# Banded attention followed by a two-layer feed-forward: 64-key tiles, longer load rows, a second load queue and a column-split last tile

## The chip, the cores and the metric

The kernel runs on one core of a Trainium2 chip. Its time is device microseconds (us) of one execution. The names of the engines are those of the profile: PE multiplies matrices (TensorE), PEld loads its weights, ACT is ScalarE, DVE is VectorE, POOL is GpSimd, SP is SyncE. A "unit" is one step of attention, a "block" a run of tokens that goes through the feed-forward together.

## The reference

Eight sequences of 576 tokens, eight heads of 64; attention reaches 32 tokens to each side. The 4608 x 512 result goes through a feed-forward with a squared relu. All inputs and the output are float32. Cut to what matters:

```python
def _attn_ref(q, k, v):                       # each (8, 8, 576, 64)
    scores = (1 / np.sqrt(D)) * np.matmul(q, k.transpose(0, 1, 3, 2))
    mask = np.abs(pos[:, None] - pos[None, :]) <= 32
    ...                                       # softmax over the masked scores
    return np.matmul(attn, v)

def _moe_ref(x, w_in, w_out, s, b):           # x (4608, 512), w_in (512, 2048), w_out (2048, 512)
    r = np.maximum(x @ w_in, 0.0)
    g = s * (r * r) + b
    return g @ w_out                          # s and b are single numbers
```

The constant b is taken out of the product: the kernel adds b times the column sums of w_out at the end.

## The kernel before

All work is declared as tasks. A planner with assumed durations puts them in an order, each engine runs its list, and semaphores join the lists. Loads bring one block of tokens with all heads, so that every contiguous piece in memory is one token of one head, 256 bytes:

```python
        def load(b, n, blk, stream="sp", waits=()):
            ...
                lambda e: e.dma_start(
                    STG[n][p0:p1, blk, :].rearrange("p (h d) -> p h d", h=H),
                    src_of[n][b, :, s0:s0 + ns, :].rearrange("h s d -> s h d"),
                ),
```

Weights come through GpSimd's queue, which casts them to bfloat16 on the way. A unit is 192 queries of four heads, with 128 keys a tile, so there are 8 x 3 x 2 = 48. Its softmax sums are a matrix product with ones, and the division is exp(-ln(sum)) on ACT:

```python
        def unit(b, t, g2, after):
            ...
                        fns.append(lambda e, u=u, pr=pr, a=a, hh=hh: e.matmul(
                            SC[:, hh, 256 * u + 128 * a:256 * u + 128 * a + 128],
                            lhsT=KT[slot][64 * hh:64 * hh + 64, pr, q0 + 128 * a:q0 + 128 * a + 128],
                            rhs=QT[slot][64 * hh:64 * hh + 64, pr, q0 + 64 * a:q0 + 64 * a + 128],
                            start=True, stop=True))
            ...                                # exp on ACT with bias=ZERO_F[:, :], mask on DVE
            for (dst, res) in ((SS, "SS"), (AV, "AV")):
                ...                            # SS: lhs = ONES, AV: lhs = VB; 8 matmuls each
            add("act", lambda e: e.activation(LNS[e_][:, :], SS[:, 0:384], AF.Ln,
                                              bias=ZERO_F[:, :], scale=1.0),
            ...
            add("act", lambda e: e.activation(REC[e_][:, :], LNS[e_][:, :], AF.Exp,
                                              bias=ZERO_F[:, :], scale=-1.0),
            ...                                # DVE: XT = AV * REC
```

The feed-forward takes blocks of 384, 128 and then 512 tokens. A first product (w_in), relu on ACT, square on DVE, and a second product (w_out) a 128-token tile at a time:

```python
    sizes = [384, 128]
    while sum(sizes) < T:
        sizes.append(min(512, T - sum(sizes)))
    ...
        for m in range(NM + 1):
            if m < NM:
                for ft in range(16):
                    s1(m, ft)
            if m == 0:
                colsum()
            else:
                for sub in range(TBLK[m - 1][1] // 128):
                    for qd in range(4):
                        s2(m - 1, sub, qd)
```

The softmax here doesn't subtract the row's maximum and nothing guards it: scores larger than these inputs give would overflow.

Of the kernel before, what the change touches and what calls it, by code (L numbers as in the profile page):

```python
# [17 lines left out]
NBLK = (S + 127) // 128  # L18
KCOLS = NBLK * 128
TOK = 512  # L20
# [4 lines left out]
class _Task:  # L25


    __slots__ = ("n", "stream", "fns", "cost", "lat", "key", "deps", "after", "users", "left",
                 "ready", "start", "fin", "dma", "sem", "seq", "val", "used", "snap")

    def __init__(self, n, stream, fns, cost, lat, key, dma):
        self.n, self.stream, self.fns, self.cost, self.lat, self.key, self.dma = \
            n, stream, fns, cost, lat, key, dma
        self.deps, self.after, self.users = set(), [], []
        self.ready = self.start = self.fin = 0.0
        self.sem = self.seq = self.val = None
        self.used = False
        self.snap = None


class _Graph:
# [3 lines left out]

    STREAMS = ("pe", "act", "dve", "pool", "sp")
    LAT = {"pe": 230.0, "act": 110.0, "dve": 90.0, "pool": 120.0, "sp": 60.0}

    def __init__(self, queues):
        self.queues = queues  # L50
        self.tasks = []
        self.writer, self.readers, self.named = {}, {}, {}

    def add(self, stream, fns, cost, reads=(), writes=(), key=0.0, accum=False, dma=None, waits=(),
            after=(), name=None, lat=None):


        if not isinstance(fns, list):
            fns = [fns]
        t = _Task(len(self.tasks), stream, fns, cost, self.LAT[stream] if lat is None else lat, key,  # L60
                  dma)
        t.deps.update(waits)
        for r in reads:
            assert r in self.writer, r
            t.deps.add(self.writer[r])
# [6 lines left out]
        t.after = list(after)  # L72
# [6 lines left out]
        if name is not None:  # L79
            self.named[name] = t  # L80
        self.tasks.append(t)
        return t

    def plan(self):
        free = {s: 0.0 for s in self.STREAMS}
        dma_free = 0.0
        for t in self.tasks:
            aft = [self.named[a] for a in t.after]
            t.left = len(t.deps) + len(aft)
            for d in t.deps:  # L90
                d.users.append((t, True))
            for d in aft:
                d.users.append((t, False))
        open_ = {s: [] for s in self.STREAMS}
        for t in self.tasks:
            if t.left == 0:
                open_[t.stream].append(t)
        order = []
        while len(order) < len(self.tasks):
            best = None  # L100
            for s in self.STREAMS:
                for t in open_[s]:
                    c = (max(free[s], t.ready), t.key, t.n)
                    if best is None or c < best[0]:
                        best = (c, t)
            assert best is not None, "a cycle"
            (st, _, _), t = best
            open_[t.stream].remove(t)
            t.start = st
            free[t.stream] = st + t.cost  # L110
            if t.dma is not None:
                dma_free = max(dma_free, st + 1300.0) + t.dma[1]
                t.fin = dma_free + 700.0
            else:
                t.fin = st + t.cost
            order.append(t)
            for u, hard in t.users:
                u.left -= 1
                if hard and u.stream == t.stream and t.dma is None and t.stream == "pe":
                    r = t.fin  # L120
                elif hard:
                    r = t.fin + (100.0 if t.dma is not None else t.lat)
                else:
                    r = t.start
                u.ready = max(u.ready, r)
                if u.left == 0:
                    open_[u.stream].append(u)
        self.order = order

    def emit(self, sems):  # L130


# [5 lines left out]
        plan = []  # L138

# [12 lines left out]
        for t in self.order:  # L152
            s = t.stream
            need = {}
            for d in t.deps:
                if s == "pe" and d.stream == "pe" and d.dma is None:
                    continue
                want(s, d, need)
            if t.dma is not None:
# [20 lines left out]
        count = {}  # L180
        for t, waits in plan:
            if t.dma is not None:
# [6 lines left out]
            def run(eng, t=t, waits=waits):  # L189
                for d in waits:  # L190
                    eng.wait_ge(sems[d.sem], d.val)
                for i, fn in enumerate(t.fns):
                    ins = fn(eng)
                    if t.dma is not None:
# [15 lines left out]
def bass_sliding_window_symmetric__then__act_starrelu_kernel(  # L210
# [12 lines left out]
    NT3 = S // 192  # L223

    sizes = [384, 128]
# [8 lines left out]
    with ExitStack() as es:  # L234
# [6 lines left out]
        def ps(shape, nm, dt=F32):  # L241
            uid["n"] += 1
            return es.enter_context(nc.psum_tensor(f"{nm}_{uid['n']}", list(shape), dt))

        WIN_BF = sb((128, 4, DFF), BF16, "win")
        WOUT_BF = sb((128, 16, DM), BF16, "wout")
        XT = sb((128, NPAIR, T), BF16, "xt")
        STG = {n: sb((128, NBLK, DM), F32, "stg" + n) for n in "qk"}
        STG["v"] = sb((128, 2 * NT3, DM), F32, "stgv")
        NAT = {n: sb((128, NBLK, DM), BF16, "nat" + n) for n in "qk"}  # L250
        VB = [sb((128, 2 * NT3, DM), BF16, "vb") for _ in range(2)]
        QT = [sb((128, NPAIR, S), BF16, "qt") for _ in range(2)]
        KT = [sb((128, NPAIR, S + 2 * WIN), BF16, "kt") for _ in range(2)]
        EX = [sb((128, 2, 512), BF16, "ex") for _ in range(2)]
        MASK = sb((128, 2, 512), BF16, "mask")
        LNS = [sb((128, 384), F32, "lns") for _ in range(2)]
        REC = [sb((128, 384), F32, "rec") for _ in range(2)]
        ONES = sb((128, 3, 64), BF16, "ones")
        ONESW = sb((128, 128), BF16, "onesw")
        IDENT = sb((128, 128), BF16, "ident")  # L260
        ZERO_F = sb((128, 1), F32, "zero")
        GT = [sb((128, 16, 512), BF16, "gt") for _ in range(2)]
        R1 = [sb((128, 512), BF16, "r1") for _ in range(4)]
        OUTS = [sb((128, DM), F32, "outs") for _ in range(3)]
# [3 lines left out]
        W = [ps((128, 512), "w") for _ in range(2)]  # L268
        O = [ps((128, 512), "o") for _ in range(2)]
        SC = ps((128, 2, 512), "sc")  # L270
        AV = ps((128, 512), "av")
        SS = ps((128, 512), "ss")
        BANKS = {("W", 0): W[0], ("W", 1): W[1], ("O", 0): O[0], ("O", 1): O[1]}

        queues = {"w": [f"dmaW{i}" for i in range(10)], "l": [f"dmaL{i}" for i in range(24)],
                  "a": [f"dmaA{i}" for i in range(8)], "o": [f"dmaO{i}" for i in range(8)],
                  "t": [f"dmaT{i}" for i in range(8)]}
        names = list(_Graph.STREAMS) + [x for n in queues for x in queues[n]]
# [4 lines left out]
        def rows(blk):  # L283
            return min(128, S - blk * 128)


        src_of = {"q": q, "k": k, "v": v}

        def load(b, n, blk, stream="sp", waits=()):
            if n == "v":  # L290
                k0 = 192 * (blk // 2) - WIN + 128 * (blk % 2)
                p0, p1 = max(0, -k0), min(128, S - k0)
                s0 = k0 + p0
            else:
                p0, p1 = 0, rows(blk)
                s0 = 128 * blk
            ns = p1 - p0
            return add(
                stream,
                lambda e: e.dma_start(  # L300
                    STG[n][p0:p1, blk, :].rearrange("p (h d) -> p h d", h=H),
                    src_of[n][b, :, s0:s0 + ns, :].rearrange("h s d -> s h d"),
                ),
                1070.0 if stream != "pool" else 1900.0, writes=[("STG", n, blk)],
                key=16 * (b - 2), waits=waits,
# [337 lines left out]
```

## Time and profile before

| | before |
|---|---|
| time, median of 3 runs | 375.03 us (374.42 to 376.37) |
| span of the profiled run | 373.8 us |
| PE busy / idle | 319.2 / 54.6 us |
| first feed-forward matmul starts | 31.88 us |
| first 512-token block starts | 99.25 us |
| DMA packets, of them under 512 B | 127,869 / 116,672 |

Here are two more views of the kernel before. The first is the page's line of busy times. The second is the trace cut into three stretches at the start of the first 512-token block and at the end of PE's work: each line has the stretch, its length, then busy time and instruction count of PE, PEld, DVE, ACT and POOL, then granted PE clock, DMA share and GB/s.

```profile
PE 319.2 (85%) x2385; PEld 155.5 (42%) x2424; DVE 193.2 (52%) x439; ACT 206.4 (55%) x310; POOL 44.7 (12%) x62
```

```profile
0.00:99.25 99.25, 59.11 (x533) 34.88 (x538) 48.41 (x127) 44.42 (x74) 26.35 (x41) 0.88 1.13 192
99.25:370.20 270.95, 260.05 (x1853) 120.62 (x1886) 144.09 (x312) 162.00 (x236) 18.37 (x22) 0.99 0.65 123
370.20:373.80 3.60, 0.00 (x0) 0.00 (x0) 0.75 (x1) 0.00 (x0) 0.00 (x0) 0.80 0.19 73
```

The busy line alone says "PE 85%". The stretches say more: 40 of the 54.6 idle microseconds lie in the first 99.25 (99.25 - 59.11), where the DMA share is full and the clock is 0.88. In the second stretch PE is busy 96%, so there less PE work can help, and at most 11 us of idle.

### The profile page before, as it was taken

The numbers are of one execution on the slowest core, as the hardware profiler recorded it, in microseconds if no ns is written. First come the engines' busy times: TensorE is split into PE (matmuls) and PEld (weight loads), VectorE is DVE, ScalarE is ACT, GpSimd is POOL, SyncE is SP. The second block draws the span as 40 slices with busy tenths as digits, with TensorE's granted clock in tenths as the row PEclk, the third lists the DMA queues.
The fourth block names the chain that finished last, engine by engine and source line by source line (L and its number), as shares of the span: only waits on it lengthen the run. The fifth ranks groups of instructions, "written<-read, shape, count | busy, mean of one in ns | idle before, by whom it ended". The sixth has DMA issues, their size and how long they took to land.

```text
span 373.8 us, 6108 instructions
## 1 busy us (share of the span) xinstructions
PE 319.2 (85%) x2385; PEld 155.5 (42%) x2424; DVE 193.2 (52%) x439; ACT 206.4 (55%) x310; POOL 44.7 (12%) x62
## 2 busy tenths in 40 slices
PE   1277985935499999988898899989999999999996
PEld 0144543523244444443444344434444444444442
DVE  4363525745556775676585586454444453333321
ACT  1266732255368678767677576657676764434300
POOL 3012241342221210121111000000000000000000
PEclk9999998975599999999999999999999999999999
DMA  8979999999999999999899798863000001001012
GB/s 164 208 110 187 190 225 206 202 190 213 230 221 147 180 200 231 186 198 193 188 172 213 132 174 174 189 141 89 28 31 31 28 30 56 28 30 56 28 58 84
DMA packets 127869, 52.71 MB, mean 141 GB/s; under 512 B 116672, under 2 KB 120768, under 8 KB 127840
## 3 DMA queue, kind: packets, MB, share of 16 engines
q1 hardware_dynamic: 113648, 36.32, 54.2%
q0 software_dynamic: 7424, 14.29, 19.8%
q10 hardware_dynamic: 6768, 1.70, 2.7%
q8 instruction: 19, 0.31, 0.4%
q14 instruction: 10, 0.08, 0.1%
HBM read 38.80 MB, written 9.44 MB: 129 GB/s over the span
## 4 chain that ended last, share of the span: by engine, by line
PE 54%; DMA 19%; SPq 9%; DVE 7%; ACTq 3%; ACT 3%; issue 2%; DVEq 0%
PE o L543 25%; PE w L525 22%; DMA stgq<-in_q_dram 12%; DMA stgk<-in_k_dram 7%; SPq L300 6%; ACTq L300 3%; SPq L387 3%; PE ss L458 3%; PE sc L435 2%; DVE ex L445 2%; PE av L458 2%; ACT ex L442 1%; DVE xt L472 1%; DVE vb L379 1%; DVE gt L534 1%
## 5 line engine op out<-in xcount | busy, mean ns | idle before, releaser
L525 PE MATMUL w<-xt,win 128*128 128x512 bf16 (+2 forms) x624 | 146.4, 367 | 5.5 <-DVE xt L472 4.2
L543 PE MATMUL o<-wout,gt 128*128 128x512 bf16 x554 | 141.5, 382 | 6.0 <-DVE cvec L567 4.0
L525 PEld LDWEIGHTS w<-xt,win 128*128 128x128 bf16 x640 | 59.4, 100 | 71.8 <-issue 5.1
L543 PEld LDWEIGHTS o<-wout,gt 128*128 128x128 bf16 x576 | 53.2, 98 | 65.5 <-DVE cvec L567 4.2
L442 ACT ACTIVATE ex<-sc,zero 128x1024 bf16<-128x1024 f32 x48 | 53.2, 1109 | 12.1 <-PE sc L435 12.1
L445 DVE TENSOR_TENSOR ex<-ex,mask 128x1024 bf16<-128x1024 bf16 x48 | 33.0, 688 | 33.2 <-ACT ex L442 32.7
L300 POOL DMA_DIRECT2D stgv<-in_v_dram x42 | 35.7, 853 | 120.5 <-DVE vb L379 111.5
L465 ACT ACTIVATE lns<-ss,zero 128x384 f32<-128x384 f32 x48 | 27.7, 578 | 27.6 <-PE ss L458 27.5
L531 ACT ACTIVATE r_29<-w,zero 128x512 bf16<-128x512 f32 (+2 forms) x40 | 25.7, 643 | 30.7 <-PE w L525 30.6
L458 PE MATMUL ss<-ex,ones 128*64 128x128 bf16 x384 | 22.1, 244 | 20.5 <-DVE ex L445 20.1
L531 ACT ACTIVATE r_28<-w,zero 128x512 bf16<-128x512 f32 (+2 forms) x40 | 25.7, 642 | 23.1 <-PE w L525 22.6
L531 ACT ACTIVATE r_31<-w,zero 128x512 bf16<-128x512 f32 (+2 forms) x40 | 25.7, 644 | 23.0 <-PE w L525 22.0
L531 ACT ACTIVATE r_30<-w,zero 128x512 bf16<-128x512 f32 (+2 forms) x40 | 25.7, 643 | 19.2 <-PE w L525 18.8
L555 DVE SCALAR_TENSOR_TENSOR outs<-o,sb_36,cvec 128x512 f32<-128x512 f32 x36 | 26.8, 746 | 13.2 <-PE o L543 12.8
L472 DVE TENSOR_TENSOR xt<-av,rec 128x384 bf16<-128x384 f32 x48 | 26.5, 552 | 11.5 <-ACT rec L468 11.2
L379 DVE CAST natq<-stgq 128x512 bf16<-128x512 f32 (+1 forms) x40 | 17.2, 432 | 25.3 <-DMA stgq<-in_q_dram 25.0
L458 PEld LDWEIGHTS ss<-ex,ones 128*64 128x64 bf16 x384 | 13.6, 119 | 39.6 <-DVE ex L445 26.7
L468 ACT ACTIVATE rec<-lns,zero 128x384 f32<-128x384 f32 x48 | 29.3, 610 | 0.8
L435 PE MATMUL sc<-qt,kt 64*128 64x128 bf16 x384 | 21.2, 237 | 9.0 <-ACT qt L407 5.3
L534 DVE TENSOR_TENSOR gt<-r_29 128x512 bf16<-128x512 bf16 (+2 forms) x40 | 15.8, 396 | 22.7 <-ACT r_29 L531 22.7
L534 DVE TENSOR_TENSOR gt<-r_31 128x512 bf16<-128x512 bf16 (+2 forms) x40 | 15.8, 396 | 22.3 <-ACT r_31 L531 22.0
L534 DVE TENSOR_TENSOR gt<-r_30 128x512 bf16<-128x512 bf16 (+2 forms) x40 | 15.8, 394 | 18.6 <-ACT r_30 L531 18.6
(43 smaller groups left out, 134.4 us busy)
## 6 DMA issues: line engine op xcount, KB each, us to landing
out_dram<-outs SPq DMA_DIRECT2D x36, 256.0 KB, 2.3
stgq<-in_q_dram SPq DMA_DIRECT2D x31, 256.0 KB, 5.8
stgk<-in_k_dram SPq DMA_DIRECT2D x29, 256.0 KB, 6.0
stgv<-in_v_dram POOLq DMA_DIRECT2D x28, 256.0 KB, 5.7
stgv<-in_v_dram POOLq DMA_DIRECT2D x14, 192.0 KB, 5.9
win<-in_moe_w_in_dram POOLq DMA_DIRECT2D x4, 512.0 KB, 6.4
wout<-in_moe_w_out_dram POOLq DMA_DIRECT2D x4, 512.0 KB, 5.8
stgq<-in_q_dram SPq DMA_DIRECT2D x8, 128.0 KB, 5.9
```

What stands on the lines that cost most here:

```text
L300: lambda e: e.dma_start(STG[n][p0:p1, blk, :].rearrange("p (h d) -> p h d", h=H), src_of[n][b, :, s0:s0 + ns, :].rearrange("h s d -> s h d ...
L435: fns.append(lambda e, u=u, pr=pr, a=a, hh=hh: e.matmul(SC[:, hh, 256 * u + 128 * a:256 * u + 128 * a + 128], lhsT=KT[slot][64 * hh:64 * h ...
L442: add("act", lambda e: e.activation(EX[e_][:, :, :], SC[:, :, :], AF.Exp, bias=ZERO_F[:, :], scale=0.125), 1130.0, reads=["SC", "ZERO"], w ...
L445: add("dve", lambda e: e.tensor_tensor(EX[e_][:, :, :], EX[e_][:, :, :], MASK[:, :, :], ALU.mult), 700.0, reads=[("E", e_), "MASK"], write ...
L458: fns.append(lambda e, u=u, a=a, hh=hh, dst=dst, lhs=lhs: e.matmul(dst[64 * hh:64 * hh + 64, 192 * u + 64 * a:192 * u + 64 * a + 128], lhs ...
L465: add("act", lambda e: e.activation(LNS[e_][:, :], SS[:, 0:384], AF.Ln, bias=ZERO_F[:, :], scale=1.0), 600.0, reads=["SS", "ZERO"], writes ...
L468: add("act", lambda e: e.activation(REC[e_][:, :], LNS[e_][:, :], AF.Exp, bias=ZERO_F[:, :], scale=-1.0), 600.0, reads=[("LNS", e_), "ZERO ...
L472: add("dve", lambda e: e.tensor_tensor(XT[:, prs[0]:prs[1] + 1, x0:x0 + 192], AV[:, 0:384].rearrange("p (u c) -> p u c", u=2), REC[e_][:, ...
L525: add("pe", [lambda e, kc=kc: e.matmul(W[wb][:, 0:nt], lhsT=WIN_BF[:, kc, ft * 128:(ft + 1) * 128], rhs=XT[:, kc, t0:t0 + nt], start=(kc = ...
L531: add("act", lambda e: e.activation(R1[rb][:, 0:nt], W[wb][:, 0:nt], AF.Relu, bias=ZERO_F[:, :], scale=1.0), 280 + 0.82 * nt, reads=[("W", ...
L534: add("dve", lambda e: e.tensor_tensor(GT[gs][:, ft, 0:nt], R1[rb][:, 0:nt], R1[rb][:, 0:nt], ALU.mult), 160 + 0.53 * nt, reads=[("R1", rb ...
L543: add("pe", [lambda e, fc=fc: e.matmul(O[ob][:, :], lhsT=GT[gs][:, fc, sub * 128:sub * 128 + 128], rhs=WOUT_BF[:, fc, :], start=(fc == 0), ...
```

## The change

It has many parts, and it touches both stages.

- *Loads.* q and k of the first two sequences come one pair of heads at a time, nine tokens to a partition (2304-byte rows). Those of later sequences come with four tokens to a row (1 KB). v keeps 256 B. Weights come as float32 on a hardware queue and are cast on chip. The loads of the last four sequences are issued from ACT's queue (`LATE = 4`).
- *Attention.* Key tiles of 64; matmuls on 64 x 64 tiles of the array, four of which fit side by side. A column of ones beside v gives the sum, DVE takes its reciprocal. There are 38 units, each with all heads of up to 128 keys: the last five sequences form one run, so that a unit may straddle two sequences (`LONG = 3`). A visit of PE to attention does the scores of one unit and the values of the unit before it.
- *Order.* Blocks of 96, 128 and 288 tokens, then 512. The planner now models the DMA rings.
- *Tail.* The last output tile is computed and stored in two halves of 256 columns.

The core of the diff, with cuts marked by "...":

```diff
-NBLK = (S + 127) // 128
+NTILE = S // 64
+LONG = 3
+LATE = 4
+XPE = 15
...
-    sizes = [384, 128]
+    sizes = [96, 128, 288]
...
+        def load_pair(b, name, pr, key, load_key, banks, eng, slack):      # sequences 0 and 1
+            add("sp", lambda e: e.dma_start(
+                STG[si][:, 0:576],
+                src_of[name][b, 2 * pr:2 * pr + 2, :, :].rearrange("h (p i) d -> (h p) (i d)", i=ROWS)),
...
+        def piece(b, parts, key, waits):                                   # later sequences
+            add(late(b), [lambda e, name=name, t0=t0, n=n, p0=p0: e.dma_start(
+                stg[p0:p0 + n // 4, :].rearrange("p (h c) -> p h c", h=H),
+                src_of[name][b, :, t0:t0 + n, :].rearrange("h (p i) d -> p h (i d)", i=4))
...                                                    # cast, DMA transpose, gather of k on POOL:
+                    add("pool", lambda e, c=c, w=w: e.tensor_copy(
+                        KT[slot][:, :, c:c + w].rearrange("p a (s i) -> p a s i", i=4),
+                        KTR[slot][:, :, :, c // 4:(c + w) // 4].rearrange("p i a s -> p a s i")),
...
+        def qk_part(c, u):
+            fns = [lambda e, pr=pr, x=x, b=b, j=j, hp=hp: e.matmul(
+                SC[64 * x:64 * x + 64, hp, pr * 128:pr * 128 + 128],
+                lhsT=KT[b % 2][64 * hp:64 * hp + 64, pr, 64 * j:64 * j + 64],
+                rhs=q_window(b, pr, j)[64 * hp:64 * hp + 64], start=True, stop=True)
+                for pr in range(NPAIR) for x, (b, j) in enumerate(at) for hp in (0, 1)]
...
+                return [lambda e: e.matmul(                                # values, with the sum
+                    av[64 * x:64 * x + 64, h, 0:D + 1],
+                    lhsT=buf[64 * g:64 * g + 64, h % 2, h // 2, c:c + 64],
+                    rhs=VB[64 * g:64 * g + 64, (vb + j // 2 - u) % (2 * NUNIT), h, 0:D + 1], start=first, stop=True,
...
-            add("act", lambda e: e.activation(LNS[e_][:, :], SS[:, 0:384], AF.Ln,
-            add("act", lambda e: e.activation(REC[e_][:, :], LNS[e_][:, :], AF.Exp,
+            add("dve", lambda e: e.reciprocal(REC[ri][0:p1, :].rearrange("p (a one) -> p a one", one=1), av[0:p1, :, D:D + 1]),
...
-            add("act", lambda e: e.activation(R1[rb][:, 0:nt], W[wb][:, 0:nt], AF.Relu,
-                                              bias=ZERO_F[:, :], scale=1.0),
+            add("act", lambda e: e.activation(rt, wt, AF.Relu, bias=0.0, scale=1.0),
...
+        for c0 in (0, 256):
+            for qd in range(4):
+                s2(final, qd, c0=c0, cn=256, shift=c0)
```

## The prediction

> **What bounds the kernel now.** I read the page's forty slices first, then the windows by stage, the waits of PE, the chain that ended last, and last the timeline of a dense stretch for unit costs.
>
> ```profile
> PE   1277985935499999988898899989999999999996
> PEclk9999998975599999999999999999999999999999
> DMA  8979999999999999999899798863000001001012
> PE 54%; DMA 19%; SPq 9%; DVE 7%; ACTq 3%; ACT 3%; issue 2%; DVEq 0%
> ```
>
> A slice is 9.3 us. PE is short of work in the first twelve slices (to about 110 us), while the DMA row is full until about 250 us. From slice 13 on PE is at 9 with a few 8s. So there are two stages: a head limited by loads, and a body limited by PE. The chain agrees: PE holds 54%, and DMA with its queues (SPq, ACTq) 31%. The windows (PE busy, PEld, DVE, ACT, POOL, then clock, DMA share, GB/s) put numbers to it:
>
> ```profile
> 80.00:90.00 10.00, 4.90 (x72) 3.45 (x72) 6.26 (x14) 6.18 (x10) 3.19 (x4) 0.50 1.22 215
> 90.00:100.00 10.00, 3.46 (x42) 2.39 (x44) 5.20 (x13) 3.95 (x6) 1.92 (x3) 0.50 1.17 240
> 100.00:110.00 10.00, 10.00 (x41) 4.08 (x40) 6.12 (x15) 5.50 (x8) 2.55 (x3) 0.86 1.16 206
> 310.00:330.00 20.00, 19.89 (x92) 9.09 (x93) 7.22 (x15) 7.97 (x13) 0.00 (x0) 1.00 0.07 26
> 330.00:350.00 20.00, 19.89 (x93) 9.02 (x93) 6.63 (x15) 7.91 (x12) 0.00 (x0) 1.00 0.11 40
> ```
>
> At 80 to 100 us the queues are full, PE works 42% and at half clock. At 310 to 350 us PE is 99.5% busy at full clock with nothing loading. The chain shows what the head waits for, one load of q that took 16 us, and where the first 512-token block of the feed-forward begins (99.25 us). The waits show attention's own latency chain (score, exp, mask, sum), which stops PE for 2 us a unit:
>
> ```profile
> 43.01 16.09 DMA stgq<-in_q_dram
> 87.34 10.20 DMA stgq<-in_q_dram
> 99.25 6.95 PE w L525 x23
> PE ss L458 <- DVE ex L445: 20.1, 13, 2.0
> ```
>
> The unit costs come from the timeline of PE in the dense stretch:
>
> ```profile
> 250.59 1.03 PE L525 MATMUL w<-xt,win 128*128 128x512 bf16 x4
> 251.55 0.41 PE L458 MATMUL ss<-ex,ones 128*64 128x128 bf16 x8
> 251.80 0.39 PE L458 MATMUL av<-ex,vb 128*64 128x128 bf16 x8
> 252.12 1.04 PE L543 MATMUL o<-wout,gt 128*128 128x512 bf16 x4
> 252.99 1.03 PE L525 MATMUL w<-xt,win 128*128 128x512 bf16 x4
> 253.95 0.40 PE L435 MATMUL sc<-qt,kt 64*128 64x128 bf16 x8
> 254.28 1.04 PE L543 MATMUL o<-wout,gt 128*128 128x512 bf16 x4
> ```
>
> Durations overlap, so starts count. In the chain after 310 us a group of four feed-forward matmuls begins every 0.865 us: 216 ns each. From 250.59 to 252.12 is 1.53 us; less 0.865, the sums and values cost 0.665. From 252.99 to 254.28 is 1.29; less 0.865, the scores cost 0.425. A unit costs PE 1.09 us, and there are 384/8 = 48.
>
> The span then closes. Feed-forward: 9 times 512 tokens, 64 matmuls in each of two products, 1152 x 0.216 = 249. Column sum 16 x 0.216 = 3.5. Attention 48 x 1.09 = 52. PE idle 373.8 - 319.2 = 54.6. The rest, some 15, is half speed: 7 by the clock row at 60 to 110 us, 8 in the first 37 us, where eight 384-column matmuls took 2.7 us (342 ns each) against 162 ns later at 42 us. Sum 374.
>
> **What the Trainium skill says.** "DMA: Bandwidth & Descriptors", Specifications, gives 512 B as the least transfer for line rate. The trace agrees: 116,672 of 127,869 packets are under 512 B, and the head gets 215/1.22 = 176 GB/s per full share, while the tail's 2 KB output rows get 26/0.07 = 371 and 40/0.11 = 364. "TensorE: Matmul & The Clock Gate", Part 1, says PE runs at half rate until about 3.4 us of sustained activity, and that a warm matmul takes N/2.4 ns plus 2.5. Agreed: 216 ns at N = 512, and 342 against 162 at N = 384, though the clock row does not show the cold start. "TensorEngine Tiling (Array Packing)", Key Properties, says 64x64 tiles run independently, four at a time, and that changing the mode drains the array. The trace fits two tiles side by side plus a drain: 16 matmuls of 128 columns two at a time are 427 ns and cost 665; eight are 213 and cost 425. So 0.21 to 0.24 us per visit. "SBUF — State Buffer", Who interferes with whom, says GpSimd shares a port pair with VectorE; POOL computes almost nothing here, so no row tests it.
>
> **The change, part by part.** The order listing of both programs gives the counts.
>
> *Loads.* q and k of the first two sequences come in 2304-byte rows, later ones in 1 KB rows; only v keeps 256 B. Weights come on the hardware queue as f32 in 2 KB and 1 KB rows and are cast on chip (14 on POOL, 2 on DVE). All q, k and v is 28.3 MB, 3.54 per sequence. Before the second block of tokens can begin, the kernel needs two sequences (7.1 MB, of it v 2.36), w_in 4.19 and half of w_out 2.1: 13.4 MB. At my estimate of 330 GB/s for long rows and 176 for v: 11.0/0.330 + 2.36/0.176 = 33 + 13 = 46 us, plus 3 to start. Five units of attention follow, each bound by its chain (exp 1.11, mask 0.69, and three or four hand-overs, near 2.8 us), partly beside the loads of v: the first 512-token block can start at 58 to 62 us, not 99.
>
> *The first product* needs one sequence (3.54 MB, some 14 us) and one quarter of w_in. Per head pair: cast, transpose, evacuation (0.6), scores, exp 1.1, mask 0.7, ACT about 1.8 a pair. The last pair lands near 10 us, so the first tokens reach the feed-forward at about 18 us (31.88 before). Blocks of 96, 128 and 288 tokens let it start before the sequence is done.
>
> *Attention on PE.* 38 units in place of 48, no sums product (a ones column beside v). The 33 units after the first sequence have 16 scores and about 32 value matmuls: 16 x 128/4 = 512 and 32 x 65/4 = 520 columns, 0.43 us four tiles wide, plus 0.22 for the switch, plus an allowance of 0.2 for a part of the concurrency lost: 0.85. 33 x 0.85 = 28.
>
> *Added on PE.* 144 transposes of 64x64 for the second sequence: 144 x 27 ns + 8 x 0.22, about 5.6. Transposes of normalised rows for 15 units (later ones by DMA), 10 of them after the head, 10 x 0.25 = 2.5. The values of the first sequence, 3. Short matmuls (96 columns, halves of 256): 1.5.
>
> *Other engines.* ACT: 132 x 0.686 + 33 x 1.109 + smaller pieces about 30 = 157 (206 before); the log and reciprocal passes, 57 us, go. DVE: squares 61, masks 27, outputs 27, normalising 26, reciprocals 8, copies 31: 180 (193). Both have room. POOL has some 60 copies without a measured duration.
>
> *Tail.* The last evacuation takes 256 columns: about 0.35 us less of 0.75. From PE's end to the end 3.1 in place of 3.6.
>
> *Sum.* Head to the first product 18; then PE work 249 + 3.5 + 1.5 + 28 + 5.6 + 2.5 + 3 = 293; tail 3.1: 314 with no gap. Add 2 for cold clock and units arriving one by one at 18 to 23 us, and 2 to 3 for waits where w_in quarters and the second sequence arrive: **318**. A second way: block start at 60, then 16 x 13.8 = 221, what is left of the first 512 tokens' second product 6, 28 units 24, tail 3, waits 3: 317.
>
> **Rivals.** *POOL takes the place of the DMA:* 24 gathers of k and most casts stand between a load and its unit. If they run beside DVE at double time, units come late and PE waits. For: the shared port. Against: sequences are loaded well ahead, and a sequence's 35 us of PE time is far more than its POOL work. 325 to 340. *Small matmuls do not pack:* at 53 and 27 ns one after another a unit is 0.85 + 0.87 + 0.22 = 1.9 us, adding 36: 352. Against: the trace's two-wide packing is complete but for the drain. *The head does not shrink:* if loads stay near 215 GB/s, 13.4 MB take 62 us and the block starts at 75: 330. Against: 371 per share on long rows. *ACT or DVE as bound:* 157 and 180 of 318; no. *Better than I think:* units of 0.7 and no waits, 309.
>
> **Range and chances.** Even two rivals together (POOL late and a slow head) stay under 350, so faster is nearly sure. 318, range 309 to 331. Faster 0.97, same 0.02, slower 0.01.
>
> **What would show it.** Right: first w matmul at 16 to 20 us; 512-column ones by 65 us; PE busy tenths at 9 from slice 8; a unit's visit to PE 0.75 to 1.0 us between feed-forward starts; DMA under full share after 65 us; tail 3 us. Wrong: PE waits on nat, kt or vb from POOL above 5 us in sum; a unit over 1.2 us; the clock at 0.5 after 70 us; DMA near full share through the body.

## The result, and the profile after

The changed kernel took 319.49 us in the median of six runs (317.63 to 320.71), the kernel before in the same rounds 375.69 (373.34 to 377.08). The ratio is 0.859, 95% interval 0.8525 to 0.8658. A ratio here is the mean time of one kernel's fast runs over that of the other's of the same rounds, so it is not quite the ratio of the medians. A run more than 1.5% above the fastest of its kernel counts as slow and is left out. On a second chip the ratio was 0.848. The prediction was 318, with 309 to 331 as its range.

The page after: busy times, then the slices of PE, PE clock and DMA share (a slice is now 8.0 us), then the chain that ended last.

```profile
PE 296.8 (93%) x3429; PEld 164.1 (52%) x3468; DVE 198.3 (62%) x380; ACT 139.3 (44%) x217; POOL 84.4 (27%) x100
...
PE   2788997999999999999999999999999999999995
...
PEclk9999999799999999999999999999999999999999
DMA  7999999997997899499979995999222110000021
...
PE 73%; DMA 3%; DVE 2%; issue 2%; POOL 1%; ACT 1%; POOLq 0%; SPq 0%
```

PE reaches 9 in the fifth slice, drops to 7 in the seventh and stays at 9 from the eighth, as the prediction said, nearly all of it at full clock. The two chains that ended last can't be compared share by share: the one before begins at 2.08 us, the one after only at 56.23 us, since the program followed it no further back (its shares add up to 82%). Its 73% of PE and 3% of DMA say that PE sets the pace from there on; they say nothing of the head. The 55.5 us that the span lost are 33.1 of PE idle (54.6 less 318.3 - 296.8 = 21.5) and 22.4 of PE busy (319.2 - 296.8).

The same three stretches in the changed kernel, with the first cut once more at the first feed-forward matmul:

```profile
0.00:18.89 18.89, 10.38 (x309) 8.53 (x309) 11.37 (x27) 10.43 (x14) 8.87 (x25) 1.00 0.93 269
18.89:67.62 48.73, 44.17 (x774) 35.36 (x770) 30.29 (x62) 22.35 (x41) 25.51 (x29) 0.96 1.04 292
67.62:314.90 247.28, 242.21 (x2353) 120.20 (x2390) 156.14 (x292) 106.50 (x162) 49.99 (x47) 1.00 0.72 151
314.90:318.30 3.40, 0.00 (x0) 0.00 (x0) 0.48 (x1) 0.00 (x0) 0.00 (x0) 1.00 0.12 40
```

The head shrank by 31.6 us (99.25 to 67.62) and the body by 23.7 (270.95 to 247.28); the tail gave 0.2. Data rates in the head rose from 192 to 269 and 292 GB/s.

The body gained in two ways, which the singly recorded matmuls divide. Before, PE stands still five times for more than 0.2 us, 7.3 us in sum; in the changed kernel never. Its 5.0 us of idle are gaps of 0.16 us where records are missing (969 of the feed-forward matmuls of 512 columns are in this trace; the run with tiles in series has 1008, and 0.1 us of idle in its body). So about 7 of the 23.7 us were idle and about 16 are PE work. By unit costs, attention in the body fell from 36 x 1.09 = 39 us to 27 x 0.75 = 20 (288 old score matmuls at eight a unit, 432 new ones at sixteen), while 3.5 us of the first 512 tokens' second product moved into it.

A visit of PE to attention, from the timeline of PE (start, length, what, idle before it):

```profile
162.64 1.03 PE L938 MATMUL o<-wout,gt 128*128 128x512 bf16 x4
163.60 0.32 PE L709 MATMUL avn<-vb,ex 64*64 64x65 bf16 x16
163.75 0.39 PE L651 MATMUL sc<-qt,kt 64*64 64x128 bf16 x16
164.00 0.32 PE L709 MATMUL avn<-vb,ex 64*64 64x65 bf16 x16
164.47 1.67 PE L920 MATMUL w<-xt,win 128*128 128x512 bf16 x7 [0.16 <-issue]
```

Four feed-forward matmuls take 0.865, so the visit starts at 163.505. A w group is eight matmuls, but only seven are in the trace: the first record is missing, and its start was 164.47 - 0.216 = 164.25. The "0.16 issue" is that missing record and not a wait. The visit cost 0.75 us, where the prediction said 0.85. The single records behind these lines show the four tiles: the scores start in fours, at 163.752, 163.756, 163.758 and 163.762 us, and the next four from 163.807 on, 55 ns later.

The waits of PE (what waited, for what: us in sum, times, longest), and the longest of them in the timeline:

```profile
PE w L562 <- ACT nat L555: 4.4, 1, 4.4
PE w L920 <- issue: 2.4, 15, 0.2
PE o L961 <- POOL wout L508: 2.3, 1, 2.3
...
PE w L562 <- POOL nat L556: 1.1, 1, 1.1
```

```profile
56.37 3.33 PE L961 MATMUL o<-wout,onesw 128*128 128x256 bf16 x16 [2.31 <-POOL wout L508]
```

```profile
53.65 1.04 POOL L508 CAST wout<-stg 128x1024 bf16<-128x1024 f32 x1 [1.80 <-DMA stg<-in_moe_w_out_dram]
55.16 1.06 POOL L508 CAST wout<-stg 128x1024 bf16<-128x1024 f32 x1 [0.47 <-DMA stg<-in_moe_w_out_dram]
```

The 4.4 is the start of the kernel, before anything has arrived. At 54.06 us PE stops for the cast of the last part of w_out. The two lines of GpSimd show that its last two casts had waited for their loads. So of the stop of 2.31 us some 1.1 are a late load and 1.06 its cast. The column sum that follows runs cold, that is at a lower clock (7 in the PEclk row): 3.33 us for 16 matmuls that took 1.92 at 36.73 us. All waits for POOL add up to 4.1.

Two rows of groups (busy us, mean ns of one, idle before):

```profile
L927 ACT ACTIVATE r<-w 128x512 bf16<-128x512 f32 x132 | 78.6, 597 | 105.9 <-PE w L920 92.4 <-DVE outs L951 12.4 <-DVE gt L929 0.4
L929 DVE TENSOR_TENSOR gt<-r 128x512 bf16<-128x512 bf16 x132 | 68.0, 522 | 64.1 <-ACT r L927 63.5
```

The relu became cheaper (686 ns before) and the square dearer (422 before). Neither was in the prediction.

### The profile page after: what moved, and what is told of

Its sections match the earlier page's. It is cut to its first block, busy times and chain, and to the rows that moved or that the text cites. A ratio compares the mean times of both kernels' runs of the same rounds, so it can differ in the third digit from the quotient of the medians.

```text
span 318.3 us, 8129 instructions
## 1 busy us (share of the span) xinstructions
PE 296.8 (93%) x3429; PEld 164.1 (52%) x3468; DVE 198.3 (62%) x380; ACT 139.3 (44%) x217; POOL 84.4 (27%) x100
## 2 busy tenths in 40 slices
DMA packets 104531, 56.69 MB, mean 178 GB/s; under 512 B 77040, under 2 KB 96240, under 8 KB 104496
## 4 chain that ended last, share of the span: by engine, by line
PE 73%; DMA 3%; DVE 2%; issue 2%; POOL 1%; ACT 1%; POOLq 0%; SPq 0%
PE o L938 34%; PE w L920 32%; PE avn L709 3%; DMA ktr<-nat 3%; PE sc L651 2%; POOL kt L617 1%; PE o L961 1%; DVE nat L600 1%; ACT r L927 1%; DVE ex L683 1%; PE avn L740 0%; DVE xn L733 0%; ACT ex L679 0%; POOLq L1011 0%; DVE outs L951 0%
## 5 line engine op out<-in xcount | busy, mean ns | idle before, releaser
L920 PE MATMUL w<-xt,win 128*128 128x512 bf16 (+3 forms) x678 | 140.1, 344 | 4.1 <-issue 2.4
L938 PE MATMUL o<-wout,gt 128*128 128x512 bf16 (+1 forms) x643 | 140.2, 353 | 2.6 <-issue 1.3
L927 ACT ACTIVATE r<-w 128x512 bf16<-128x512 f32 (+2 forms) x152 | 87.0, 575 | 115.8 <-PE w L920 100.9
L929 DVE TENSOR_TENSOR gt<-r 128x512 bf16<-128x512 bf16 (+2 forms) x152 | 77.9, 520 | 69.3 <-ACT r L927 68.5
L617 POOL COPY kt<-ktr 128x512 bf16<-128x512 bf16 (+1 forms) x30 | 31.6, 1054 | 49.3 <-DMA ktr<-nat 47.8
L679 ACT ACTIVATE ex<-sc 128x1024 bf16<-128x1024 f32 (+1 forms) x33 | 33.8, 1023 | 22.1 <-PE avn L709 20.4
L951 DVE SCALAR_TENSOR_TENSOR outs<-o,sb,cvec 128x512 f32<-128x512 f32 (+1 forms) x41 | 27.9, 681 | 21.6 <-PE o L938 21.5
L600 POOL CAST nat<-stg 128x1024 bf16<-128x1024 f32 (+1 forms) x21 | 23.6, 1122 | 63.1 <-DMA stg<-in_q_dram 34.9
L683 DVE TENSOR_TENSOR ex<-ex,mask 128x1024 bf16<-128x1024 bf16 (+1 forms) x33 | 25.7, 779 | 1.8
L733 DVE TENSOR_TENSOR xn<-avn,rec 128x512 bf16<-128x512 f32 (+1 forms) x32 | 22.1, 689 | 0.9
L651 PE MATMUL sc<-qt,kt 64*64 64x128 bf16 x504 | 13.4, 216 | 0.0
```

The lines of the kernel that those rows point to most:

```text
L600: add(eng, lambda e, x=x: e.tensor_copy(nat[0:top, 1024 * x:1024 * x + 1024].rearrange("p (i h d) -> p h i d", h=H, i=2), stg[0:top, :].re ...
L617: add("pool", lambda e, c=c, w=w: e.tensor_copy(KT[slot][:, :, c:c + w].rearrange("p a (s i) -> p a s i", i=4), KTR[slot][:, :, :, c // 4: ...
L651: fns = [lambda e, pr=pr, x=x, b=b, j=j, hp=hp: e.matmul(SC[64 * x:64 * x + 64, hp, pr * 128:pr * 128 + 128], lhsT=KT[b % 2][64 * hp:64 * ...
L679: add("act", lambda e, dst=flat_dst, src=flat_src: e.activation(dst, src, AF.Exp, bias=0.0, scale=0.125), 190 + 0.833 * 512 * len(hs), rea ...
L683: add("dve", lambda e, flat=flat, mask=mask: e.tensor_tensor(flat, flat, mask, ALU.mult), 130 + 0.53 * 512 * len(hs), reads=[("E", ei, hp, ...
L733: add("dve", lambda e: e.tensor_tensor(XN[xi][0:p1, :].rearrange("p (a c) -> p a c", a=H), av[0:p1, :, 0:D], REC[ri][0:p1, :].rearrange("p ...
```

## The experiments

Twelve kernels ran, in three calls. The first call was on one chip, the second and third on another, where the changed kernel itself was run again. Differences are against its 318.9 us, and are only good to some microseconds for the first call, which ran on the other chip. There the kernel before scattered from 370.38 to 377.99 us, five of its eleven runs counted as slow, and the verdicts are marked unclear.

| kernel | call | median of fast runs, us | ratio to before [95%] | against 318.9 |
|---|---|---|---|---|
| kernel before, long rows | 1 | 360.2 | 0.9645 [0.957, 0.972] | |
| short rows | 1 | 328.8 | 0.880 [0.872, 0.888] | +9.9 |
| tiles in series | 1 | 322.3 | 0.865 [0.856, 0.874] | +3.4 |
| late column sum | 1 | 318.0 | 0.851 [0.846, 0.856] | -0.9 |
| changed kernel again | 2 | 318.9 | 0.848 [0.845, 0.851] | 0 |
| whole tail | 2 | 318.9 | 0.848 [0.845, 0.851] | 0.0 |
| one queue | 2 | 322.5 | 0.858 [0.853, 0.862] | +3.6 |
| gather on ACT | 2 | 324.7 | 0.865 [0.860, 0.870] | +5.8 |
| two tiles | 3 | 332.6 | 0.885 [0.881, 0.890] | +13.7 |
| short late rows | 3 | 356.9 | 0.948 [0.942, 0.953] | +38.0 |
| zero bias | 3 | 319.6 | 0.850 [0.847, 0.853] | +0.7 |
| no straddling | 3 | 323.4 | 0.862 [0.857, 0.866] | +4.5 |

The theory: the head lost its idle time because rows are longer and work starts earlier; the body lost what the smaller units save on PE, because four tiles work side by side; nothing else counts. Its rivals are named with each run.

### Long rows in the kernel before

q and k are read in 2 KB rows in the old kernel. The tokens then land in the wrong places, so its attention is wrong. The comparison with the reference says little about attention with inputs this small.

```diff
+                dst = STG[n][p0:p1, blk, :]
+                src = src_of[n][b].rearrange("h (s x) d -> (h s) (x d)", x=8)[s0:s0 + ns, :]
```

> The kernel before with q and k read as whole 2 KB rows (as many bytes into the same tiles, so the result is wrong on purpose), everything else as it was. It isolates the row length of q and k. Theory: the head is limited by the time of the 256 B packets; q and k of the two sequences that the second block of tokens needs are 4.7 MB, at 176 GB/s 27 us and at some 350 GB/s 13, so that block begins some 13 us before 99.25 us and the time falls by 10 to 16 us, to about 362 us. Rival 1: the row length is the whole head: the block begins near 68 us, as in the changed kernel, and the time falls to 345 us or less. Rival 2: the rows do not matter, since the issuing queues or the attention chain hold the head: 371 us or more.

Measured: 360.2 us, about 14 less than before. The first product starts at 27.68 us (31.88), the first 512-token block at 91.66 (99.25). Packets fall to 63,357. So 7.6 us come in the head and the rest of the 15.7 between the two spans (373.8 and 358.1) after it, where the old kernel also stopped for loads: in its body PE stood still for 7.3 us, with long rows not once for 0.2 us. The row length of q and k by itself is worth this much to the old kernel, and no more: its block still starts 24 us later than the changed kernel's.

### Short rows for the first two sequences

The other way round: the changed kernel with its first two sequences of q and k in 256-byte pieces, the values right.

```diff
-                STG[si][:, 0:576],
-                src_of[name][b, 2 * pr:2 * pr + 2, :, :].rearrange("h (p i) d -> (h p) (i d)", i=ROWS)),
+                STG[si][:, 0:648].rearrange("p (i c) -> p i c", c=72)[:, :, 0:64],
+                src_of[name][b, 2 * pr:2 * pr + 2, :, :].rearrange("h (p i) d -> (h p) i d", i=ROWS)),
```

> The changed kernel with q and k of the first two sequences landing in 256 B pieces (a stride of 72 elements in the staging tile in place of 64; same bytes, right result). Theory: each sequence's 2.36 MB take some 6 us longer, so the first product begins at 24 to 26 us in place of 18.9, the first 512-token block at 78 to 82 us in place of 67.6, and the time is 329 to 333 us. Rival: the head is held by weights and by the chain of the units, not by these rows: first product under 21 us, time 318 to 322 us.

Its stretches, cut at the first product and at the first 512-token block:

```profile
0.00:23.04 23.04, 10.68 (x309) 8.33 (x309) 13.13 (x27) 10.48 (x14) 9.21 (x25) 1.00 1.03 222
23.04:75.94 52.90, 42.80 (x776) 33.76 (x769) 30.69 (x61) 22.46 (x41) 24.79 (x29) 0.97 1.04 262
75.94:327.30 251.36, 247.54 (x2399) 120.39 (x2392) 156.50 (x293) 106.44 (x162) 49.35 (x47) 1.00 0.72 150
```

The first stretch grows by 4.2 us and the second by 4.2, the rest by 0.7 (251.36 against 247.28 + 3.40). That is the whole loss, and it stands where the theory puts it: rows of the first two sequences are worth 8 to 9 us of the head, a little under what was expected. The rates fell from 269 and 292 to 222 and 262 GB/s. The edit also makes the casts read with a stride (on DVE 754 ns in the mean against 474), but DVE's wait for loads of k before them doubled, from 4.5 to 9.3 us, so the loads are the larger part. The other 23 us of the head's 31.6 are not from these rows. Candidates are the longer rows of later sequences, the weights on a hardware queue, the earlier start, the finer blocks and the feed-forward work mixed between units; these were not tried one by one. Rate times time gives 19.1 MB moved up to the first 512-token block before (19.9 with long rows), 19.0 here and 19.3 in the changed kernel. The bytes are nearly the same, so the head's length goes with the data rate (192, 217, 250 and 285 GB/s on average); that the rate alone sets it is not shown. What raised the rate from 192 to 250 between the kernel before and this one stays open.

### The order of the tiles in a visit

All matmuls of one tile are put one after another instead of alternating.

```diff
-                for pr in range(NPAIR) for x, (b, j) in enumerate(at) for hp in (0, 1)]
+                for x, (b, j) in enumerate(at) for hp in (0, 1) for pr in range(NPAIR)]
```

The order of the value matmuls is changed in the same way.

> The changed kernel with the scores and value matmuls in another order: four in a row on the same 64x64 tile of PE in place of four different ones; same work, right result. Theory: the 0.75 us of a unit's visit to PE come from four tiles working side by side. One after another a unit takes 16 x 53 + 32 x 27 = 1.7 us and the drain, so some 1.8 us, 33 units add 33 x 1.0 and the time is 345 to 358 us. Rival: tiles do not overlap in time and a visit is set by issue or by loading weights: visit 0.75 us still, time 318 to 322 us.

```profile
163.38 1.03 PE L938 MATMUL o<-wout,gt 128*128 128x512 bf16 x4
164.34 0.34 PE L709 MATMUL avn<-vb,ex 64*64 64x65 bf16 x15
164.49 0.21 PE L651 MATMUL sc<-qt,kt 64*64 64x128 bf16 x1
164.50 0.19 PE L709 MATMUL avn<-vb,ex 64*64 64x65 bf16 x1
164.52 0.43 PE L651 MATMUL sc<-qt,kt 64*64 64x128 bf16 x15
164.81 0.35 PE L709 MATMUL avn<-vb,ex 64*64 64x65 bf16 x16
165.10 1.90 PE L920 MATMUL w<-xt,win 128*128 128x512 bf16 x8
```

A visit takes 165.10 - 164.245 = 0.855 us instead of 0.75, and 33 visits (the units after the first sequence) times 0.105 are 3.5 us, near the table's 3.4, which compares two chips. My theory of what this would show fell: I had expected the four tiles to be lost, at 1.8 us a visit. The order in which tiles are called matters little: the lines show a score that starts at 164.49 us, before the last value matmul, which stands ahead of it in the program, at 164.50, so a tile that is free does not wait for its neighbours' turn. So this run did not test the packing at all, and another had to.

### Two tiles instead of four

Every attention matmul of the later units uses the first 64 rows of the array, so that only two tiles are in use. The number and size of matmuls stay. The values are wrong.

```diff
-                lhsT=KT[b % 2][64 * hp:64 * hp + 64, pr, 64 * j:64 * j + 64],
-                rhs=q_window(b, pr, j)[64 * hp:64 * hp + 64], start=True, stop=True)
+                lhsT=KT[b % 2][0:64, pr, 64 * j:64 * j + 64],
+                rhs=q_window(b, pr, j)[0:64], start=True, stop=True)
```

The operands of the value matmuls lose their `64 * g` in the same way.

> The changed kernel with every score and value matmul of the units after the first sequence taking its operands from partitions 0 to 63 (wrong heads and tokens on purpose), so that two 64x64 tiles of PE are used in place of four; the number and size of matmuls stay. The run with four matmuls in a row on one tile gave 0.855 us a visit, not 1.8, so order alone does not serialise. Theory: each tile has its own line of work, and what counts is the work on the fullest tile: 8 x 53 + 16 x 27 = 0.86 us on each of two tiles in place of 0.43 on each of four, a visit of 1.05 to 1.2 us, 33 x 0.35 = 11 us more: 328 to 333 us. Rival: a visit is set by issue (some 15 ns a matmul whatever the tile), 0.75 to 0.85 us, time 318 to 322.

```profile
152.15 1.89 PE L938 MATMUL o<-wout,gt 128*128 128x512 bf16 x8
...
154.25 0.61 PE L651 MATMUL sc<-qt,kt 64*64 64x128 bf16 x16
...
155.27 1.67 PE L920 MATMUL w<-xt,win 128*128 128x512 bf16 x7 [0.16 <-issue]
```

The eight matmuls end at 152.15 + 1.73 = 153.88, and with its missing record the next group starts at 155.05: 1.17 us a visit, 0.42 more. 33 x 0.42 = 13.9, and the time rose by 13.7. In the single records the scores now start in pairs, 55 ns from pair to pair. This shows the mechanism: each tile works through its own matmuls, and four of them at once are what a visit of 0.75 us rests on.

It does not show that four tiles are why a unit is cheaper than before: by the prediction's reading the old matmuls filled the array too, two at a time on tiles of twice the size. By its count of columns, an estimate, the columns fell from 48 x 0.64 = 31 us to 33 x 0.43 = 14, since the sums product went and fewer masked keys are computed, and the rest of the visits (1.09 - 0.64 and 0.75 - 0.43) from 22 to 11, since visits are fewer and shorter. No run took these apart.

### The second column sum later

The planner is told that casts of the second half of w_out end 4 us later, so that it plans the column sum behind them.

```diff
-                key=key + 150.0, slack=100.0)
+                key=key + 150.0, slack=4000.0 if which == "out" and x else 100.0)
```

> The changed kernel with one number of its plan changed: the second half of w_out is taken to come 4 us later, so the second column sum stands behind two more units' work on PE. In the changed kernel PE waits 2.3 us at 54 us for a cast of that half and then runs cold: the sum takes 3.3 us where the first took 1.9. Theory: both go, and the time falls by 3 to 4 us, to 315 to 316.5 us (ratio to the kernel before some 0.849). Rival: the wait only moves (the units of the second sequence are what holds the block, and it still begins at 67 us): 318 to 320 us.

The stop is gone from the trace and the block starts at 65.83 us. The time is 318.0, but on the other chip, and the changed kernel's own second profile shows a wait of 1.3 us there, a column sum that is not cold, and a block start at 66.42, without any edit. So the wait comes and goes by itself. The medians say 0.9 us better, the ratios (0.851 against 0.848) say worse. The run is inconclusive.

### The changed kernel again

> The changed kernel itself again, as the reference for the runs beside it on the same chip: 318 to 321 us.

It took 318.9 us (318.37 to 319.47), ratio 0.848. This is the reference for the second and third call.

### The last tile whole

```diff
-        for c0 in (0, 256):
-            for qd in range(4):
-                s2(final, qd, c0=c0, cn=256, shift=c0)
+        for qd in range(4):
+            s2(final, qd)
```

> The changed kernel with its last output tile in one piece in place of two column halves. Theory: the last evacuation takes 0.75 us in place of 0.48 and the last store is twice as long, so from the end of PE to the end of the span there are 3.6 to 3.8 us in place of 3.4, against 0.1 us saved on PE by fewer matmuls: 0.1 to 0.4 us more, not separable from noise by the times alone (0.1%), to be read in the trace. Rival: the split is worth a us or more.

The time is the same within 0.1 us. From the start of the last evacuation to the end of the span the profile has 3.3 us here and 3.4 with the halves. The evacuation is 0.27 us shorter with halves (0.48 against 0.75), but the last store then takes 2.92 us instead of 2.55, where I had expected the whole tile's store to be the longer. So this part of the change is worth nothing that can be measured.

### All loads on one queue

```diff
-LATE = 4
+LATE = 8
```

> The changed kernel with all loads issued from the one queue of SyncE (those of the last four sequences came from ScalarE's). Theory: from 70 us on PE is the bound at 98 to 99% busy and the loads run ahead, so another issuer changes nothing that PE sees: 318 to 322 us. Rival: loads block transposes and stores behind them in one queue, units come late and PE waits: 325 us or more, with PE busy under 97% at 110 to 230 us.

322.5 us in the fast runs, 3.6 more; one run of 328.21 counted as slow. The time lies between the two statements. PE is busy 113.8 of the 120 us from 110 to 230 (116.9 with two queues), with single waits of 0.9 us for a mask and 1.8 us for a square; the rival's second sign, under 97%, came true. In the chain, loads of k take 7%; in the changed kernel's chain they are not among the lines shown. The second queue is worth some 4 us, not more.

### The gathers of k on ACT

This asks why DVE's squares went from 422 to 522 ns. If GpSimd's copies hold them up, they must get faster when GpSimd does less.

```diff
-                    add("pool", lambda e, c=c, w=w: e.tensor_copy(
+                    add("act", lambda e, c=c, w=w: e.copy(
```

> The changed kernel with the 30 gathers of k moved from GpSimd to ScalarE. The squares on VectorE take 522 ns in the mean where they took 422 in the kernel before, and casts 609 where they took 436, with GpSimd busy 84 us instead of 45. Theory: they share a way into memory with GpSimd's copies, and with 32 us of these gone the squares' mean falls to some 470 to 495 ns; the time stays at 317 to 321 us because VectorE is not the bound. Rival 1: the squares are slow for another reason: still 515 to 530. Rival 2: the gathers on GpSimd hold the units: the time falls by over 2 us.

Squares of the same shape, and ACT's timeline from 75 us on:

```profile
L929 DVE TENSOR_TENSOR gt<-r 128x512 bf16<-128x512 bf16 x132 | 58.3, 446 | 66.4 <-ACT r L927 65.7
```

```profile
75.45 4.53 ACT L617 COPY kt<-ktr 128x512 bf16<-128x512 bf16 x5
79.89 1.01 ACT L679 ACTIVATE ex<-sc 128x1024 bf16<-128x1024 f32 x1
```

Squares fall to 446 ns and casts of v from 609 to 416 (436 in the kernel before), so GpSimd's copies are what made most of DVE's work slower; by what way they meet, the run does not show. But DVE was not the bound, and the time rose by 5.8 us: ACT runs five gathers in a row ahead of an exp, and PE then waits 2.4 us for the mask behind it. With two more stops of 0.8 and 0.6 us that is 3.8 us; the rest was not placed. The expectation for the squares held (a little better than its 470 to 495), that for the time did not.

### Short rows in the later sequences

The loads of sequences 2 to 7 are split into four DMAs of 256-byte pieces each.

```diff
-                src_of[name][b, :, t0:t0 + n, :].rearrange("h (p i) d -> p h (i d)", i=4))
-                for name, t0, n, p0 in parts],
+                src_of[name][b, :, t0:t0 + n, :].rearrange("h (p i) d -> p h i d", i=4)[:, :, i, :])
+                for name, t0, n, p0 in parts for i in range(4)],
```

> The changed kernel with the loads of q and k of the last six sequences (1 KB rows) split into four, each of 256 B rows: same bytes, right result, four times the issues. Theory: in the body a sequence's 3.5 MB at 256 B rows take some 20 us of every 35 us of PE time; loads still run ahead and PE stays at 98%: 318 to 323 us. Rival: the long rows of the later sequences are what keeps the body on PE; units come late and PE waits: 328 us or more.

My theory, that body loads are hidden anyway, fell by a wide margin: 356.9 us, 38 more. The timeline of ACT and its queue shows how:

```profile
110.41 4.34 ACTq L592 DMA_DIRECT2D stg<-in_q_dram  x4
114.79 1.08 ACT L927 ACTIVATE r<-w 128x512 bf16<-128x512 f32 x2 [5.78 <-issue]
```

Four issues hold ACT's instruction stream for 4.34 us, and no relu and no exp runs meanwhile: ACT was idle 5.78 us. In the changed kernel one issue of 1 MB from ACT takes 0.37 to 0.43 us, though two issues of v took 3.66 us together at 150.76 us, without a stop of PE. In this run PE waits 12.4 us in sum for relus and 11.6 for masks, and ACT's queue alone takes 14% of the chain. The block start is all but unchanged (68.2 us). Two things were changed at once, the rows (133,489 packets under 512 B against 77,040) and the number of issues. Which of them lengthens the issues is left open. What is shown is the way of the loss: while an issue lasts, the engine that issues it does nothing else.

### A bias tile for the activations

```diff
-            add("act", lambda e: e.activation(rt, wt, AF.Relu, bias=0.0, scale=1.0),
+            add("act", lambda e: e.activation(rt, wt, AF.Relu, bias=ZERO_F[:, :], scale=1.0),
```

Both exps were changed in the same way.

> The changed kernel with the activations' bias given as a tile of zeros, as in the kernel before, in place of the constant 0.0. It asks why the relu of 128x512 takes 597 ns now and took 686, and the exp of 1024 columns 1024 against 1109. Theory: the bias tile costs some 85 ns an activation: relu 680 to 690 ns again, exp 1105 to 1112, and the time does not move (318 to 321 us) since ScalarE is not the bound. Rival: the durations differ for another reason and stay at 597 and 1024.

A relu takes 687 ns instead of 597, an exp 1114 instead of 1024, and ACT is busy 155.3 us instead of 139.3. The time does not move (319.6). So the constant bias explains ACT's 139 where 157 was predicted, and it is not on the path.

### No unit across sequences

```diff
-LONG = 3
+LONG = 8
```

> The changed kernel with every sequence cut into units of its own (40 units) in place of one run of units through the last five sequences (38 units, some with the end of one sequence and the start of the next). Theory: two more visits of 0.75 us and their exps and masks: 1 to 3 us more, 320 to 322 us. Rival: units are hidden anyway or the boundaries matter more than the count: no change, or over 4 us.

323.4 us in the fast runs, 4.5 more; one run of 330.44 counted as slow. A line of PE's timeline:

```profile
149.77 0.44 PE L709 MATMUL avn<-vb,ex 64*64 64x65 bf16 x16 [2.37 <-DVE ex L683]
```

Two more units cost 2 x 0.75 = 1.5 us. The rest is waits like this one, and loads of k in 9% of the chain: with another plan, units of attention come late. The expected 1 to 3 us was too little, as it counted PE's work alone.

None of these versions beats the changed kernel by more than the scatter.

## Why the prediction was right

The total was right by a sum in which single terms missed both ways. The sum was 18 to the first product, 293 of PE work, 2 of cold clock, 2.5 of waits and 3.1 of tail: 318.6. Measured on the span of 318.3: 18.9; then 286.4 of PE busy and 9.6 idle to 314.9; then 3.4. Of the idle, the 5.0 us after 67.62 are missing records, as said above (486 of the 512 w matmuls of 512 columns are in the trace). So work was about 291 and idle about 4.6, all of it in the head.

- **Head to the first product: right.** 18 predicted, 18.89 measured.
- **First 512-token block at 58 to 62 us: wrong, at 67.62.** The main term that failed is the chain of five units, sized at 14 us (five of 2.8). PE's visits to the second sequence's units start at 46.9, 50.1, 52.8, 60.3 and 63.9 us, and the next at 66.8: some 20 us, of which 7.5 for the unit that has the stop for w_out and the cold column sum. Without that stop, in the run with the later column sum, they took 17.4 us (47.8 to 65.2), so the units themselves were undersized too. The load term failed as well: it counted half of w_out, 13.4 MB in 49 us, but the plan's column sum needs all of it, and by 53.9 us 16.3 MB had been moved (303 GB/s) with the last of w_out just landing. The late block cost little, since PE was busy 44.17 of these 48.73 us with the first 512 tokens' feed-forward. At the block's start 32 half-width matmuls of their second product (3.5 us) were left, near the 6 us that the second way of summing allowed. Where PE has other work, a late block start is not a loss of the same size.
- **A unit's visit of 0.85: 0.75.** The allowance of 0.2 us for lost concurrency was half unneeded; 33 x 0.10 = 3.3 us. That four tiles work side by side, as the prediction assumed, is shown by the run with two tiles.
- **Transposes of the second sequence, 5.6: 3.0.** 36 of them take 0.7 us, four times, once 1.0. I had counted them one after another, at 27 ns each plus two switches a pair.
- **Cold clock and waits, 4.5 together: more.** The cold column sum added 1.4 us, and idle after the first product is about 4.6 where 2 to 3 were allowed. These, with 0.9 us in the first product and 0.3 in the tail, make up for much of the two terms above, which is luck: 293 - 3.3 - 2.6 + 1.4 = 288.5, plus the 2 of cold clock that the prediction listed apart, is 290.5, near the 291 of work.
- **Other engines: right in kind, both sizes off.** ACT 157 predicted, 139.3 measured, through the constant bias. DVE 180 predicted, 198.3 measured, of which the slower squares are 132 x 0.1 = 13, mostly through GpSimd's copies. Neither is on the path.
- **Tail: right in kind.** 3.1 predicted, 3.4 measured; the split's gain went into a slower last store.
- **"DMA under full share after 65 us": wrong.** From 70 to 200 us the share is 1.03 at 206 GB/s. Yet PE is busy 126.8 of these 130 us. A full share alone did not bind.
- **"Sequences are loaded well ahead": too generous.** One queue (+3.6) and no straddling (+4.5) made PE wait in the body, with loads of k in 7% and 9% of the chain, and short late rows (+38) far more. Loads are early enough in the plan as it stands, but with little to spare.

The rivals: small matmuls that do not pack are excluded by the visit of 0.75 us; a head that does not shrink, by its 31.6 us; GpSimd in place of the DMA, by 4.1 us of waits for it, about half of the longest of which was a late load; ACT or DVE as the bound, by their 44% and 62%. What stays open is how the head's gain beyond the rows of the first two sequences divides among the other loads, the earlier start, the block sizes and the mixing, how the cheaper units divide among fewer columns and fewer visits, and which half of the edit in the short late rows cost the 38 us.

## What to carry to other kernels

Cut the profile into stages and ask in each whether PE is idle or busy: here the head held most of the idle time, and in the body two thirds of the gain were less PE work. Small matmuls are cheap when they spread over independent tiles of the array, so count columns divided by tiles, plus a switch, and do not count instructions. A queue on a computing engine gives a little as long as its issues go straight through, and costs much once they block.

## What the Trainium skill lacked or had wrong

- "TensorE: Matmul & The Clock Gate", Part 1: it puts the least time from one matmul's start to the next at about 25 ns. Here 16 score matmuls on four 64 x 64 tiles start within 0.25 us, 15.6 ns each, and 48 matmuls with the switches take 0.75 us. The floor does not hold across tiles, which Part 1 does not say (a later part of the page does treat tiles side by side).
- "TensorEngine Tiling (Array Packing)", Key Properties: it says that tiles are independent, but not whether the order of instructions matters, and this page gives the speedup of tiles only as theory. Here: alternating 0.75 us, tile after tile 0.855, two tiles 1.17 for the same 48 matmuls.
- "DMA: Bandwidth & Descriptors", Issuing engines are not separate DMA queues: it says that issuing from several engines saves only the issue time, usually small. A second queue saved 3.6 us of 322.5 here. It lacks the reverse: four issues held ScalarE's stream for 4.34 us, and the kernel with four times as many issues on shorter rows lost 38 us.
- "SBUF — State Buffer", Who interferes with whom: it names the port shared by GpSimd and VectorE, and the runs agree that the two slow each other, but it gives no size for such copies and squares. Squares of 128 x 512 took 422 ns before, where 35.7 of GpSimd's 44.7 us were DMA issues, 522 with it busy for 84 us, and 446 with its gathers taken away.
